# Gated linear attention with a channel mix: later loads for part of the weights and for the decays

## The chip, the cores and the metric

One NeuronCore of a Trainium2 chip runs the whole program. The metric is the device time of one execution in microseconds (us). TensorE (PE) does matmuls, VectorE (DVE), ScalarE (ACT) and GpSimd (POOL) work on tiles, and every transfer is issued by SyncE (SP), in the order in which its instructions stand, onto 16 DMA engines that share them.

## The reference

```python
def _attn_ref(q, k, v, f_logit):           # (4, 8, 768, 48) each
    f = 1.0 / (1.0 + np.exp(-f_logit))
    state = zeros(B, H, D, D)
    for t in range(S):
        state = f[:, :, t, :, None] * state + einsum('bhd,bhe->bhde', k[:, :, t], v[:, :, t])
        y[:, :, t] = einsum('bhd,bhde->bhe', q[:, :, t], state)

def _moe_ref(x, mu_k, mu_r, w_k, w_v, w_r):  # x = y as (4, 768, 384), d_ff = 1024
    x_prev = x shifted by one step
    xk = mu_k * x + (1 - mu_k) * x_prev
    xr = mu_r * x + (1 - mu_r) * x_prev
    k = maximum(xk @ w_k, 0)
    return sigmoid(xr @ w_r) * (k * k @ w_v)
```

Inputs and output are float32.

## The kernel before, in words

The 4 x 768 steps are cut into 24 chunks of 128 steps (`i`), six to a batch row; three chunks make a unit (`u`, 8 of them). A chunk is attention work (`add_attention`, L215), a unit is the mix and the three weight products (`add_mix`, L454). The work is written as named tasks with their engines, estimated costs, places and dependencies, and a planner (`Plan.schedule`, L84) picks one task after another by the earliest start that its own estimates give; the instructions of each engine then stand in that order. A task that gets a new dependency thus changes the order of others on every engine, and the number of filler matmuls.

The tasks of chunk `i` that matter here: `qk` loads q and k (512 KB, four buffers, so chunk 4 takes chunk 0's), `v` loads v (192 KB, three buffers); `b` scans the decays into running products; `q`, `kr`, `n`, `k` scale q and k (L250 to L272; `kr` on GpSimd, L258 and L259); `TR` transposes the keys on PE and `kt` copies them out (L314 and L315); `SP` makes scores and state sums (L325, L345); `m` masks the scores (L337), `za`, `zb`, `T` carry the state (L290, L296, L302); `YA` and `YB` are the output matmuls (L362), `w` lies between them (L381 and L382), `y` copies the result out (L394 on ScalarE or L396 on VectorE). The results of three chunks are spread into x by six small transfers (`sp`, L452).

The tasks of unit `u`: `d`, `xm`, `xh`, `xl` make the mixed inputs as a high and a low part (L464 to L497); `F0` to `F7` multiply by 128 columns of wk each (L505), `r`, `h`, `kk`, `l` square the relu into high and low parts (L528 to L543); `R0` to `R2` multiply by wr, `W` by wv in two halves; `sg` takes the sigmoid of that and of the decays of unit `u + 3` (L568, L571), `o` and `out` finish. `f{u}` loads the decays of a unit (768 KB, three buffers, L410).

Weights come as 64-bit words that are turned into a high and a low float part on the chip (`add_words`, L601). wk has 8 pieces of 384 KB (piece p is what F`p` reads), wv 6 of 512 KB through two buffers, wr 4. A piece is a load (L629), three VectorE steps S, T, X (L623, L632, L635), a ScalarE cast of the high part (L638) and the low part on GpSimd (L642). Late in the program the words are loaded again to be checked (`add_check`, L682), through the same two buffers.

Where the planner finds PE without work it puts in filler matmuls in fours (`fill`, L697).

Of the kernel before, what the change touches and what calls it, by code (L numbers as in the profile page):

```python
# [18 lines left out]
P = 128  # L19
# [3 lines left out]
UC = 3  # L23
# [8 lines left out]
NQ, NFB = 4, 3  # L32
# [159 lines left out]
class Rwkv:  # L192


    wk = wr = wv = None
# [205 lines left out]
    def add_unit(self, pl, u):  # L401

        nc = self.nc
        gates = [f"{n}{i}" for i in range(UC * (u - NFB), UC * (u - NFB + 1)) for n in "bg"
                 if i >= 0 and (n == "b" or i % NCH > 0)]
        ga = u - LEAD - GATE
        t = lambda cs=slice(0, UC): self.f_t[u % NFB][:, cs]

        def load(cs=slice(0, UC)):
            nc.sync.dma_start(self.f_t[u % NFB][:, cs], self.zt[u, :, cs])  # L410

        if u == 0:
            for c in range(UC):
                cs = slice(c, c + 1)
                pl.add(f"f0.{c}", ga - 0.4, ("Q", 0.71, 1, lambda cs=cs: load(cs)))
                pl.add(f"sf0.{c}", ga - 0.4, ("A", 0.63, 0, lambda cs=cs: nc.scalar.activation(t(cs), t(cs), AF.Sigmoid)),
                       after=[f"f0.{c}"] + ([f"sf0.{c - 1}"] if c else []))
        else:
            pl.add(f"f{u}", ga - 0.4 if u >= NFB else -1.5 + 0.1 * u, ("Q", 2.13, 1, load), after=gates)
            if u < NFB:  # L420
                def sf():
                    nc.scalar.activation(t(), t(), AF.Sigmoid)
                    if SPLIT and u == 2:
                        nc.scalar.preload_act_table_set(EXP_SET)

                pl.add(f"sf{u}", -1.0 if SPLIT and u == 2 else -9, ("A", 1.5 + 2.6 * (SPLIT and u == 2), 0, sf),
                       after=[f"f{u}", ("ex" if SPLIT else "sf1") if u > 1 else "sf0.2"])
            else:
                pl.add(f"sf{u}", u - 2.5, ("A", 0.0, 0, lambda: None), after=[f"sg{u - NFB}"])
        x, s = lambda: self.b("x", u), lambda: self.b("stage", u)  # L430
        ys = [f"y{i}" for i in range(UC * u, UC * u + UC)]
        for j in range(KJ):
            pl.add(f"sp{u}.{j}", u - PREP - 0.1, ("Q", 0.2, 2, lambda j=j: self.spread(x(), s(), j)), after=ys, uses=[("x", u), ("stage", u)])
        if u % NU == 0:
            pl.add(f"x0{u}", u - PREP, ("G", 0.1, 0, lambda: nc.gpsimd.memset(x()[:, :, 0:1], 0.0)),
                   uses=[("x", u)])
        else:
            pl.add(f"x0{u}", u - PREP, ("G", 0.36, 0, lambda: nc.gpsimd.tensor_copy(
                x()[:, :, 0:1], self.b("x", u - 1)[:, :, UT : UT + 1])),
                after=[f"sp{u - 1}.{j}" for j in range(KJ)], uses=[("x", u), ("x", u - 1)])  # L440
# [160 lines left out]
    def add_words(self, pl, clamp=False):  # L601
# [3 lines left out]
        nc = self.nc  # L605

        def piece(name, p, home, view, load, shape, hi, lo, first):
            place = WORDS[name][0] + WORDS[name][1] * p
            n = int(np.prod(shape))
            us = lambda per, at: per * n + at  # L610
            t_key = ("pm", (name, p))

            def t(dt=I32):
                a = self.b(*t_key)[:, :n].bitcast(dt)
                return a if len(shape) == 1 else a.rearrange("p (a b) -> p a b", a=shape[0])

            def shift():
                high = view()[..., 1]
                if clamp:
                    nc.scalar.activation(t(F32), high.bitcast(F32), AF.Abs)  # L620
                    nc.vector.tensor_scalar(t(F32), t(F32), 2.0**-15, None, op0=ALU.max)
                    high = t()
                nc.vector.tensor_scalar(  # L623
                    t(), high, 3, 0x3FFFFFFF, op0=ALU.logical_shift_left, op1=ALU.bitwise_and)

            low, high = lambda: view()[..., 0], lambda: view()[..., 1]
            x = lambda: low().bitcast(F32)
            tu = {"takes" if first else "uses": [home]}
            pl.add(f"{name}{p}", place - 0.4, ("Q", n * P * 8 / 370e3, 1, lambda: nc.sync.dma_start(view(), load())), **tu)  # L629
            dve = us(0.00104, 0.15)  # L630
            pl.add(f"{name}S{p}", place, ("V", dve, 0, shift), after=[f"{name}{p}"], takes=[t_key], uses=[home])
            pl.add(f"{name}T{p}", place, ("V", dve, 0, lambda: nc.vector.scalar_tensor_tensor(  # L632
                t(), low(), 29, t(), op0=ALU.logical_shift_right, op1=ALU.bitwise_or)),
                after=[f"{name}S{p}"], uses=[t_key, home])
            pl.add(f"{name}X{p}", place, ("V", dve, 0, lambda: nc.vector.scalar_tensor_tensor(  # L635
                low(), high(), -0x40000000, t(), op0=ALU.bitwise_and, op1=ALU.bitwise_or)),
                after=[f"{name}T{p}"], uses=[t_key, home])
            pl.add(f"{name}H{p}", place, ("A", us(0.00104, 0.12), 0, lambda: nc.scalar.copy(hi(), x())),  # L638
                   after=[f"{name}X{p}"], uses=[home])

            def sub(e):
                e.tensor_tensor(lo(), x(), hi().bitcast(F32), op=ALU.subtract)  # L642

            pl.add(f"{name}L{p}", place, ("G", us(0.00214, 0.2), 0, lambda: sub(nc.gpsimd)),
                   ("V", us(0.00104, 0.15), 1, lambda: sub(nc.vector)), after=[f"{name}H{p}"], uses=[home])


        for i, tag in enumerate(("k2h0", "k2l0", "k2h1", "k2l1")):
            for h in range(2):
                c = slice((2 * i + h) * P, (2 * i + h + 1) * P)  # L650
                home = ("words", ("wk", 2 * i + h)) if clamp else (tag, "w")

                def view(tag=tag, h=h, home=home):
                    if clamp:
                        w = self.b(*home)[:, : 2 * DM].bitcast(I32)
                        return w.rearrange("p (a n t) -> p a n t", a=KJ, t=2)
                    return self.words[tag][:, :, h * P : (h + 1) * P]

                piece("wk", 2 * i + h, home, view, lambda c=c: self.wk[:, :, c], [KJ, P],
                      *(lambda c=c, a=a: self.w["wk"][a][:, :, c] for a in (0, 1)), clamp or h == 0)  # L660
        nq = KJ * DM // 4
        for p in range(4):
            home = ("words", ("wr", p)) if clamp else ("lg", "w") if p < 2 else ("x", "w")
            at = 0 if clamp else p % 2 * nq

            def view(home=home, at=at):
                w = self.b(*home)
                w = w if len(w.shape) == 2 else w.rearrange(FL)
                return w[:, 2 * at : 2 * (at + nq)].bitcast(I32).rearrange("p (n t) -> p n t", t=2)

            c = slice(p * nq, (p + 1) * nq)
            piece("wr", p, home, view, lambda c=c: self.wr.rearrange("p a b t -> p (a b) t")[:, c], [nq],
                  *(lambda c=c, a=a: self.w["wr"][a].rearrange("p a b -> p (a b)")[:, c] for a in (0, 1)),
                  clamp or p % 2 == 0)
        for p in range(6):
            c = slice(p * 512, (p + 1) * 512)
# [5 lines left out]
    def add_check(self, pl):  # L682

        nc = self.nc
        pieces = [(w, slice(c, c + m)) for w, n, m in ((self.wk, KJ * DFF, 512), (self.wv, NF * DM, 512), (self.wr, KJ * DM, DM))
                  for c in range(0, n, m)]
        for p, (w, c) in enumerate(pieces):
            n = c.stop - c.start
            v = lambda p=p, n=n: self.b("words", ("c", p))[:, : 2 * n].bitcast(I32).rearrange("p (n t) -> p n t", t=2)
            pl.add(f"c{p}", CHECK[0] + CHECK[1] * p, ("Q", n * P * 8 / 370e3, 1, lambda v=v, w=w, c=c: nc.sync.dma_start(  # L690
                v(), w.rearrange("p a b t -> p (a b) t")[:, c])), takes=[("words", ("c", p))])
            pl.add(f"cm{p}", CHECK[0] + CHECK[1] * p + 1, ("V", 0.00104 * n + 0.15, 0, lambda v=v, p=p: nc.vector.tensor_reduce(
                self.least[:, p : p + 1], v()[..., 1].bitcast(F32), axis=mybir.AxisListType.X, op=ALU.min,
                apply_absolute_value=True)), uses=[("words", ("c", p))])
        return [f"cm{p}" for p in range(len(pieces))]
# [249 lines left out]
```

## Time and profile before

| | us |
|---|---|
| median of 3 runs | 357.24 (357.2 to 357.62) |
| profiled execution | 357.22 |
| its span | 355.1 |
| PE busy | 320.0 (90% of the span) |
| DVE busy | 260.3 (73%) |
| ACT busy | 201.5 (57%) |
| POOL busy | 196.5 (55%) |

The span is from the first to the last instruction of the profiled execution; some 2 us lie around it. Engines run side by side, so busy times don't add up; what an engine waits for is read from the stretch in which it waits. Matmul counts are passes: a float32 matmul that isn't marked otherwise shows as two.

### The profile page before, as it was taken

The numbers are of one execution on the slowest core, as the hardware profiler recorded it, in microseconds if no ns is written. First come the engines' busy times: TensorE is split into PE (matmuls) and PEld (weight loads), VectorE is DVE, ScalarE is ACT, GpSimd is POOL, SyncE is SP. The second block draws the span as 40 slices with busy tenths as digits, with TensorE's granted clock in tenths as the row PEclk, the third lists the DMA queues.
The fourth block names the chain that finished last, engine by engine and source line by source line (L and its number), as shares of the span: only waits on it lengthen the run. The fifth ranks groups of instructions, "written<-read, shape, count | busy, mean of one in ns | idle before, by whom it ended". The sixth has DMA issues, their size and how long they took to land.

```text
span 355.1 us, 10862 instructions
## 1 busy us (share of the span) xinstructions
PE 320.0 (90%) x4482; PEld 304.0 (86%) x4482; DVE 260.3 (73%) x526; ACT 201.5 (57%) x400; POOL 196.5 (55%) x235
## 2 busy tenths in 40 slices
PE   0294678999999999999999999999999999999993
PEld 0283567888989999999999999999999999999992
DVE  7887699989998798877999788848973943723110
ACT  3786358758367827844467537772676156605520
POOL 2555459985779357733677267725790634634400
PEclk9999899999999999999999999999999999999998
DMA  7999462336451363366323632131401100010001
GB/s 260 398 378 372 162 223 65 106 105 209 118 185 59 127 226 129 123 236 221 117 81 116 212 128 89 46 121 52 160 1 38 50 27 11 9 46 22 3 24 52
DMA packets 20650, 45.32 MB, mean 128 GB/s; under 512 B 2928, under 2 KB 13040, under 8 KB 20592
## 3 DMA queue, kind: packets, MB, share of 16 engines
q1 hardware_dynamic: 20592, 44.55, 37.0%
q8 instruction: 37, 0.61, 0.7%
q14 instruction: 21, 0.17, 0.1%
HBM read 38.64 MB, written 4.72 MB: 122 GB/s over the span
## 4 chain that ended last, share of the span: by engine, by line
PE 68%; DVE 13%; ACT 5%; issue 4%; DMA 3%; POOL 3%; SPq 1%; DVEq 0%; POOLq 0%; ACTq 0%
PE pm L505 55%; PE py L362 6%; PE pm L310 3%; PE pss L325 2%; DMA f<-in_zt 2%; DVE pm L632 2%; PE pss L345 2%; DVE pm L623 2%; POOL k2l L543 1%; DVE xm L482 1%; DVE ss L337 1%; DMA words<-in_wv 1%; DVE xm L477 1%; DVE words L635 1%; DVE xh L491 1%
## 5 line engine op out<-in xcount | busy, mean ns | idle before, releaser
L505 PE MATMUL pm<-xh,wk 128*128 128x384 f32 x384 | 105.3, 344 | 1.5 <-POOL wk L642 1.1
L505 PE MATMUL pm<-wv,k2h 128*128 128x384 f32 x384 | 98.6, 338 | 0.0
L543 POOL TENSOR_TENSOR k2l<-kk,k2h 128x384 fp32r<-128x384 f32 x64 | 68.5, 1075 | 32.2 <-DVE kk L535 16.3
L497 POOL TENSOR_TENSOR xl<-xm,xh 128x384 fp32r<-128x384 f32 x48 | 52.5, 1095 | 60.4 <-DVE xh L491 54.6
L505 PEld LDWEIGHTS pm<-xh,wk 128*128 128x128 f32 x384 | 69.8, 188 | 4.4 <-POOL wk L642 2.0
L505 PEld LDWEIGHTS pm<-wv,k2h 128*128 128x128 f32 x384 | 68.7, 188 | 0.3
L505 PE MATMUL pm<-xl,wk 128*128 128x384 f32 x192 | 64.6, 337 | 0.0
L505 PE MATMUL pm<-wv,k2l 128*128 128x384 f32 x192 | 64.5, 336 | 0.0
L528 ACT ACTIVATE r<-pm 128x384 f32<-128x384 f32 x54 | 26.5, 490 | 34.0 <-PE pm L505 33.3
L505 PE MATMUL pm<-wr,xh 128*128 128x384 f32 x144 | 38.0, 345 | 1.0 <-DVE words L635 0.9
L505 PEld LDWEIGHTS pm<-wv,k2l 128*128 128x128 f32 x192 | 36.1, 188 | 0.0
L595 DVE TENSOR_TENSOR o<-pm,lg 128x384 f32<-128x384 f32 x24 | 13.3, 553 | 31.1 <-PE pm L505 30.9
L505 PEld LDWEIGHTS pm<-xl,wk 128*128 128x128 f32 x192 | 36.1, 188 | 0.0
L535 DVE SCALAR_TENSOR_TENSOR kk<-pm,r 128x384 f32<-128x384 f32 x38 | 21.1, 554 | 20.0 <-ACT r L528 18.8
L533 ACT ACTIVATE k2h<-r 128x384 fp32r<-128x384 f32 x64 | 33.6, 524 | 3.5 <-DVE r L529 1.2
L240 DVE TENSOR_TENSOR_SCAN pm<-f,low 128x512 f32<-128x512 f32 x24 | 32.7, 1363 | 0.1
L362 PE MATMUL py<-qk,z 64*64 64x64 f32 x704 | 22.9, 230 | 10.0 <-issue 3.3
L362 PEld LDWEIGHTS py<-qk,z 64*64 64x64 f32 x704 | 16.4, 135 | 18.0 <-issue 8.8
L505 PEld LDWEIGHTS pm<-wr,xh 128*128 128x128 f32 x144 | 25.2, 188 | 1.9 <-DVE words L635 1.0
L482 DVE SCALAR_TENSOR_TENSOR xm<-pm,mu_sb,x 128x384 f32<-128x384 f32 x42 | 25.7, 612 | 0.7
L700 PE MATMUL py<-ident 128*128 128x64 f32 x72 | 10.8, 310 | 15.4 <-DMA ident<-in_cst 15.4
L505 PE MATMUL pm<-wr,xl 128*128 128x384 f32 x72 | 24.2, 336 | 0.0
(101 smaller groups left out, 559.2 us busy)
## 6 DMA issues: line engine op xcount, KB each, us to landing
qk<-in_qkt SPq DMA_DIRECT2D x24, 512.0 KB, 4.3
words<-in_wv SPq DMA_DIRECT2D x12, 512.0 KB, 3.9
f<-in_zt SPq DMA_DIRECT2D x7, 768.0 KB, 5.2
v<-in_vt SPq DMA_DIRECT2D x24, 192.0 KB, 3.1
out<-o SPq DMA_DIRECT2D x24, 192.0 KB, 2.6
words<-in_wk SPq DMA_DIRECT2D x6, 512.0 KB, 5.4
words_k2h<-in_wk SPq DMA_DIRECT2D x4, 384.0 KB, 8.6
words_k2l<-in_wk SPq DMA_DIRECT2D x4, 384.0 KB, 9.4
```

What stands on the lines that cost most here:

```text
L240: pl.add(f"b{i}", ga, ("V", 1.25, 1, lambda: nc.vector.tensor_tensor_scan(b().rearrange(FL), f().rearrange(FL), self.low.rearrange(FL), 1. ...
L310: nc.tensor.transpose(pk()[:, j], k()[:, j], self.ident)
L362: first[c, h] = nc.tensor.matmul(to, lhs, rhs, start=(c, h) not in first, stop=stop, skip_group_check=True)
L482: pl.add(f"xm{u}.{n}{j}", pr, ("V", 0.62, 0, lambda xm=xm, n=n, j=j: nc.vector.scalar_tensor_tensor(xm(), pm("d", u, j)[:, :UT], self.mu_s ...
L497: e.tensor_tensor(lo(), xm(), hi().bitcast(F32), op=ALU.subtract)
L505: nc.tensor.matmul(ps, lhs(a, j), rhs(bb, j), start=ends[0] and i == 0, stop=ends[1] and i == len(pr) - 1)
L528: pl.add(f"r{u}.{f}", kf, ("A", 0.5, 0, lambda r=r, ps=ps: nc.scalar.activation(r(), ps(), AF.Relu)), ("V", 0.56, 0, lambda r=r, ps=ps: nc ...
L533: pl.add(f"h{u}.{f}", kf, ("A", 0.53, 0, lambda r=r, hi=hi: nc.scalar.activation(hi(), r(), AF.Square)), after=[f"r{u}.{f}"], **kw)
L535: pl.add(f"kk{u}.{f}", kf, ("V", 0.56, 0, lambda r=r, ps=ps, kk=kk: nc.vector.scalar_tensor_tensor(kk(), ps(), 0.0, r(), op0=ALU.max, op1= ...
L543: e.tensor_tensor(lo(), kk(), hi().bitcast(F32), op=ALU.subtract)
L595: pl.add(f"o{u}.{t}", kv, ("V", 0.56, 0, lambda t=t, ps=ps, o=o: nc.vector.tensor_tensor(o(), ps(), lg()[:, t], op=ALU.mult)), after=[f"W{ ...
L700: self.nc.tensor.matmul(self.py[:, 0, 256:320], self.ident, self.ident[:, :64], start=False, stop=True, skip_group_check=True)
```

## The change

wk pieces 4 to 7 and wv pieces 1 to 5 may be placed only after the load of q and k of chunk 5. The load of the decays of unit 4 and of each later unit is placed only after the copy of the transposed keys of chunk 3(u - 3) + 4, which is chunk 7 for unit 4. The check loads are placed only after wv piece 5.

```diff
@@ add_unit
-            pl.add(f"f{u}", ga - 0.4 if u >= NFB else -1.5 + 0.1 * u, ("Q", 2.13, 1, load), after=gates)
+            pl.add(f"f{u}", ga - 0.4 if u >= NFB else -1.5 + 0.1 * u, ("Q", 2.13, 1, load), after=gates + ([f"kt{UC * (u - NFB) + 4}"] if u > NFB else []))
@@ add_words, piece
-            pl.add(f"{name}{p}", place - 0.4, ("Q", n * P * 8 / 370e3, 1, lambda: nc.sync.dma_start(view(), load())), **tu)
+            behind = ["qk5"] if not clamp and (name == "wk" and p >= 4 or name == "wv" and p >= 1) else []
+            pl.add(f"{name}{p}", place - 0.4, ("Q", n * P * 8 / 370e3, 1, lambda: nc.sync.dma_start(view(), load())),
+                   after=behind, **tu)
@@ add_check
-                v(), w.rearrange("p a b t -> p (a b) t")[:, c])), takes=[("words", ("c", p))])
+                v(), w.rearrange("p a b t -> p (a b) t")[:, c])), after=["wv5"], takes=[("words", ("c", p))])
```

Two lines are added, so that a line after L629 has a number higher by one to two in the changed kernel.

On SyncE, the loads from wk pieces 2 and 3 (`words_k2l0`) on. In the kernel before:

```order
L629 DMA words_k2l0_130<-in_wk 128x3x256 x2
L629 DMA words_k2h1_131<-in_wk 128x3x256
L629 DMA words1_121<-in_wv 128x1024
L629 DMA words_k2h1_131<-in_wk 128x3x256
L629 DMA words_k2l1_132<-in_wk 128x3x256 x2
L230 DMA v0_101<-in_vt 128x384
L228 DMA qk0_64<-in_qkt 128x1024
L230 DMA v1_102<-in_vt 128x384
L228 DMA qk1_65<-in_qkt 128x1024
L410 DMA f1_62<-in_zt 128x1536
L230 DMA v2_103<-in_vt 128x384
```

In the changed kernel:

```order
L630 DMA words_k2l0_130<-in_wk 128x3x256 x2
L230 DMA v0_101<-in_vt 128x384
L228 DMA qk0_64<-in_qkt 128x1024
L230 DMA v1_102<-in_vt 128x384
L228 DMA qk1_65<-in_qkt 128x1024
L630 DMA words_k2h1_131<-in_wk 128x3x256
L630 DMA words1_121<-in_wv 128x1024
L630 DMA words_k2h1_131<-in_wk 128x3x256
L630 DMA words_k2l1_132<-in_wk 128x3x256 x2
L230 DMA v2_103<-in_vt 128x384
L452 DMA x1_105<-stage0_107 16x384 x6
```

The buffers `words_k2h1` and `words_k2l1` hold wk pieces 4 to 7, `words1` wv piece 1. v of chunk 3 (`v0`), q and k of chunk 4 (`qk0`), v of chunk 4 (`v1`) and q and k of chunk 5 (`qk1`) now stand ahead of them, and the decays of unit 4 (`f1`) are gone from here.

On VectorE, from the state update of chunk 2 on, between the scan of chunk 5's decays and the mix of unit 0. In the kernel before:

```order
L302 TENSOR_TENSOR sm_77<-pss_87,z01_73 128x192
L623 TENSOR_SCALAR pm1_92<-words_k2h0_129 128x384
L632 SCALAR_TENSOR_TENSOR pm1_92<-words_k2h0_129,pm1_92 128x384
L382 COPY done_76<-py_88 128x2
L635 SCALAR_TENSOR_TENSOR words_k2h0_129<-words_k2h0_129,pm1_92 128x3x128
L623 TENSOR_SCALAR pm2_93<-words0_120 128x512
L337 TENSOR_TENSOR ss1_98<-pss_87,mask_69 128x512
L296 TENSOR_TENSOR z11_75<-pss_87,z10_74 128x4x48
L302 TENSOR_TENSOR sm_77<-pss_87,z11_75 128x192
L250 TENSOR_TENSOR qk0_64<-qk0_64,pm0_91 128x512
L270 TENSOR_TENSOR pm0_91<-rb0_95,pm0_91 128x512
L262 SCALAR_TENSOR_TENSOR qk0_64<-pm0_91,qk0_64 128x2x128
```

In the changed kernel:

```order
L302 TENSOR_TENSOR sm_77<-pss_87,z01_73 128x192
L250 TENSOR_TENSOR qk0_64<-qk0_64,pm0_91 128x512
L382 COPY done_76<-py_88 128x2
L270 TENSOR_TENSOR pm0_91<-rb0_95,pm0_91 128x512
L337 TENSOR_TENSOR ss1_98<-pss_87,mask_69 128x512
L396 TENSOR_SCALAR x1_105<-py_88 128x2x128
L396 TENSOR_SCALAR x1_105<-py_88 64x128 x2
L396 TENSOR_SCALAR stage0_107<-py_88 128x128
L296 TENSOR_TENSOR z11_75<-pss_87,z10_74 128x4x48
L302 TENSOR_TENSOR sm_77<-pss_87,z11_75 128x192
L262 SCALAR_TENSOR_TENSOR qk0_64<-pm0_91,qk0_64 128x2x128
L266 SCALAR_TENSOR_TENSOR qk0_64<-pm0_91,qk0_64 128x2x64 x2
```

Here `words_k2h0` is wk piece 1 and `words0` wv piece 0. The steps of wk piece 1 and the first of wv piece 0 have gone to places behind q and k of chunks 4 and 5; the copy of chunk 2's result (L396) has come over from ScalarE.

On PE, between YB of chunk 3 and YA of chunk 4. In the kernel before:

```order
L310 MATMUL pm1_92<-ident_68,qk0_64 128x128 x4
L325 MATMUL pss_87<-qk0_64 64x64 x16
L345 MATMUL pss_87<-v1_102,ktk0_99 48x48 x16
L310 MATMUL pm1_92<-ident_68,qk1_65 128x128 x4
L700 MATMUL py_88<-ident_68 128x64 x4
```

In the changed kernel:

```order
L310 MATMUL pm1_92<-ident_68,qk0_64 128x128 x4
L310 MATMUL pm0_91<-ident_68,qk1_65 128x128 x4
L325 MATMUL pss_87<-qk0_64 64x64 x16
L345 MATMUL pss_87<-v1_102,ktk0_99 48x48 x16
L702 MATMUL py_88<-ident_68 128x64 x20
```

The transposes of chunk 5 (`qk1`) have moved ahead of the scores and sums of chunk 4, and the fillers behind these have grown from 4 to 20.

## Rows read from the trace of the kernel before

**Rows 1.** The page: PE's busy tenths in 40 slices.

```profile
PE   0294678999999999999999999999999999999993
```

**Rows 2.** Windows: length; PE, PEld, DVE, ACT, POOL busy; PEclk; DMA; GB/s.

```profile
30.00:40.00 10.00, 5.12 (x249) 4.27 (x247) 7.35 (x15) 5.46 (x15) 5.01 (x8) 1.00 0.96 335
40.00:50.00 10.00, 7.22 (x206) 6.02 (x206) 7.86 (x20) 5.23 (x13) 3.08 (x5) 0.83 0.43 143
...
100.00:110.00 10.00, 10.00 (x160) 9.37 (x159) 9.15 (x20) 7.21 (x17) 8.58 (x10) 1.00 0.34 106
```

**Rows 3.** Chain that ended last: start us, us, what.

```profile
28.59 0.78 issue
...
33.41 2.49 issue
...
41.56 1.56 PE py L362 x48
```

**Rows 4.** Windows of 1 us, columns as in rows 2.

```profile
42.00:43.00 1.00, 1.00 (x44) 0.90 (x36) 0.27 (x1) 0.00 (x0) 0.00 (x0) 0.50 0.18 43
```

**Rows 5.** Timeline of SyncE: start us, us, line, transfer, count.

```profile
20.48 0.54 SPq L629 DMA_DIRECT2D words_k2h<-in_wk  x1
...
23.57 2.50 SPq L629 DMA_DIRECT2D words_k2l<-in_wk  x2
...
27.27 0.86 SPq L228 DMA_DIRECT2D qk<-in_qkt  x1
```

**Rows 6.** DMA of 22 to 28 us: packets; issue, KB, landing us.

```profile
DMA packets 1678, 2.20 MB, mean 367 GB/s; under 512 B 80, under 2 KB 1506, under 8 KB 1677
...
qk<-in_qkt SPq DMA_DIRECT2D x1, 512.0 KB, 9.1
```

**Rows 7.** Instructions on the tile qk, 0 to 50 us.

```profile
DMA to landing us min/median/max: 3.6/6.6/9.1
```

**Rows 8.** Timeline of PE and GpSimd: start, us, what [idle before <-releaser].

```profile
33.12 0.30 PE L362 MATMUL py<-qk,z 64*64 64x64 f32 x3 [0.58 <-DVE z L296]
35.90 0.39 PE L362 MATMUL py<-qk,z 64*64 64x64 f32 x11 [2.49 <-issue]
...
36.38 0.74 POOL L258 TENSOR_TENSOR qk<-qk,rb 128x256 f32<-128x256 f32 x1 [1.65 <-DMA qk<-in_qkt]
...
40.83 0.47 PE L362 MATMUL py<-qk,z 64*64 64x64 f32 x14 [1.23 <-POOL qk L258]
```

**Rows 9.** DMA queues, 33.4 to 35.9, then 40.9 to 43 us: packets, MB.

```profile
q8 instruction: 1, 0.02, 2.7%
...
q8 instruction: 1, 0.02, 3.6%
```

**Rows 10.** Timeline of VectorE: chunk 5's result copied out.

```profile
75.12 1.04 DVE L396 TENSOR_SCALAR x<-py 128x256 f32<-128x256 f32 x3
```

**Rows 11.** Timeline of 32 to 66 us, PE.

```profile
47.91 0.46 PE L362 MATMUL py<-qk,z 64*64 64x64 f32 x16 [0.93 <-DVE z L296]
...
51.33 0.44 PE L505 MATMUL pm<-xh,wk 128*128 128x384 f32 x1
...
54.61 1.89 PE L700 MATMUL py<-ident 128*128 128x64 f32 x16
```

**Rows 12.** Timeline of GpSimd: low parts of wk 2, wk 7, wv 3.

```profile
56.53 1.03 POOL L642 TENSOR_TENSOR wk<-words_k2l,wk 128x384 fp32r<-128x384 f32 x1
...
68.83 1.02 POOL L642 TENSOR_TENSOR wk<-words_k2l,wk 128x384 fp32r<-128x384 f32 x1 [0.23 <-ACT wk L638]
...
71.06 2.33 POOL L642 TENSOR_TENSOR wv<-words,wv 128x512 fp32r<-128x512 f32 x1
```

**Rows 13.** Timeline of ScalarE: the square behind F0.0.

```profile
55.12 0.53 ACT L533 ACTIVATE k2h<-r 128x384 fp32r<-128x384 f32 x1
```

**Rows 14.** Timeline of PE: R0.1.

```profile
75.26 0.62 PE L505 MATMUL pm<-wr,xh 128*128 128x384 f32 x2 [0.87 <-DVE words L635]
```

**Rows 15.** Timeline of ScalarE: the sigmoid of unit 4's decays.

```profile
122.64 1.47 ACT L571 ACTIVATE f<-f 128x1536 f32<-128x1536 f32 x1
```

## Prediction

> **What bounds the kernel now.** I read the page's slices first, then 10 us windows, the chain of waits, and last the timeline of 14 to 100 us by engine. From slice 11 on PE is at 9 tenths in every slice but the last [rows 1], and a window there has no idle PE at all [rows 2]: after about 100 us the time is PE's work, and a change can only help by letting that stretch begin earlier. Before it PE is half idle (5.12 us of the 10 from 30 on, then 7.22), while the DMA engines are full (share 0.96, then 0.43) [rows 2]. So the question is how much earlier the first big matmul can start, and whether the start that it wins survives to 100 us.
>
> [...]
>
> **The part that is moved forward.** wk pieces 4 to 7 and wv piece 1 are 4 x 384 + 512 KB = 2.1 MB, issued from 20.48 to 26.07 [rows 5]. At the 367 GB/s of that stretch they are 5.7 us of transfer [rows 6]. q and k of chunk 4, issued at 27.27, land 9.1 us later [rows 5, 6]; the quickest such load takes 3.6 [rows 7]. Nothing else of the issue time moves: v of chunk 3 goes out just ahead of them in either order, since it waits for chunk 0's output matmuls. So chunk 4's keys land at about 31 instead of 36.4, and GpSimd's wait of 1.65 us for them [rows 8] goes. By itself that wait was not what PE waited for.
>
> PE's stall at 33.41 is. It falls after 3 of 16 passes of one task [rows 8], and a 0.02 MB packet of an instruction queue starts inside it [rows 9]. I counted the passes of the program from the start: the stalls at 28.59 [rows 3], at 33.41 and before 40.83 [rows 8] lie 126 passes apart, each a weight load and a matmul, so 252 instructions. I take each to be a wait for the next block of code, asked for when the block before it was entered. Its transfer shares the full DMA engines: from entry to entry it took 6.5 us for the block needed at 33.4 (29.4 to 35.9) and 4.9 for the next (35.9 to 40.8). With the engines nearly empty the packet after that starts within 2.1 us of the entry, and PE has no stall for it [rows 9]. [...]
>
> In the changed order the engines run nearly dry between 26.8 and 31, so that the block needed at 33.4 comes at 33.4 to 34.3; I take 33.9, a stall of 0.5. But the moved 2.1 MB now go out at 32 to 35 us, behind chunk 5's q and k, and keep the engines full to about 40. The next block is asked for at 33.9, in that stretch. With 4.0 to 6.6 us it comes between 37.9 and 40.5; I take 39.3. So **the stall is moved to the next block** more than removed.
>
> Step by step from there: YA2's rest, chunk 3's scores and sums, and YB2 end at 36.1; chunk 2's result is copied out by VectorE, 1.35 us as for chunk 5 now (1.04 us [rows 10] and a last short piece), to 37.5 (before, by ScalarE); YA3 starts and halts after two passes until 39.3 (before 40.83); YB3 ends at 41.2, at the lower clock, since PE is again idle for some 3 us, against 43.12. Term one: **-1.9 us**; bounds -3.5 (block in time, full clock) and 0.
>
> **The part that is put in between.** From YB3's end to the first matmul of unit 0's F0.0 it is 8.2 us now (43.12 to 51.33) [rows 3, 11]. In the new order chunk 4's key transposes are copied by ScalarE behind chunk 3's result, and only then come its scores: 1.35 + 0.5 + 1.3 = 3.2 us by the same tasks' lengths around 44 us. Then 20 fillers stand there instead of 4. A filler is two passes; 16 passes took 1.89 us [rows 11], so 40 take 4.7. Behind them YA4, SP5 and YB4 need 2.3 us without waits (from 47.91 to 51.33 with waits now [rows 11]). Together 10.2. VectorE is no later: piece 1 of wk now stands before the mix of unit 0, and by its steps z of chunk 4, which YA4 needs, is ready 7.4 us after YB3. Term two: **+2.0**; bounds +1.5 (VectorE alone) and +2.6 (fillers begun at the lower clock).
>
> From F0.0 to the low half of wk piece 2, which F0.2 waits for, it is 6.2 us (51.33 to 57.56 [rows 11, 12]). Now ScalarE casts wv piece 0 ahead of F0.0's relu; in the changed order the relu, which needs F0.0's end, and the square (0.53 us [rows 13]) stand first, and GpSimd's row of low halves waits for that cast: 1.6 + 0.2 + 1.1 to it, 0.7 for it, and 1.3 + 1.0 + 1.0 on GpSimd make 6.9 to 7.0. Term three: **+0.8**, bounds 0 and +1.2. From there to wk piece 7 (56.53 to 69.85) GpSimd goes from one to the next almost without a gap, in nearly the same order in both programs, so a lag is kept.
>
> Behind that there is slack. PE sits idle 0.87 us before R0.1 [rows 14], where it waits for a bank that VectorE frees, and VectorE is ahead of GpSimd in the new order; the low half of wv piece 3 took 2.33 us, where wk's, three quarters of its size, take 1.02 [rows 12]; it ran beside a scan of VectorE, which it would now miss. Term four: **-0.9**, bounds -1.0 and 0.
>
> **The rest.** The decays of unit 4 leave the full stretch and go out behind chunk 10's keys, where those of unit 5 stand now, before 100 us; the sigmoid that reads them runs at 122.64 [rows 15], so even a load of 9 us as above is covered with 10 to spare. If they slipped by more than that, ScalarE would hold unit 4. The check loads already stand behind wv piece 5. From unit 1 on PE's order is the same apart from units 4 and 5, where it changes between chunk and big matmuls twice more: **+0.2**, an estimate at 0.1 each from fractions of a microsecond of idle PE in a whole window of such changes [rows 2]; bounds 0 and 0.6.
>
> The sum is -1.9 + 2.0 + 0.8 - 0.9 + 0.2 = +0.2 us on the profiled execution's 357.22, which is within 0.02 of the median: **357.4 us**. A difference under 0.2%, 0.7 us, cannot be told from none.
>
> **Rivals.**
> (1) *The code comes in time and the clock stays up.* The request at 33.9 may meet engines that have only just filled again, or be made earlier. YB3 then ends at 39.6, and the other terms leave -1.4: 355.8 us. For it: with the engines nearly empty no block was late [rows 9]. Against: nothing was in flight then, and here 2.1 MB are. 0.30.
> (2) *The stall at 33.4 does not depend on the backlog.* If a block of code takes its turn beside the data, it took its 6.5 us for its own reasons and takes them again. Then YA2 goes on at 35.9, YB3 ends at 43.1, term one is 0, and the fillers and the new order cost their 2 us: 359.3. It decides if YA2's third pass comes after 35. [...] Against it stands that the packet ran 4 us or more after the entry at 29.4 with full engines, and within 2.1 us of the entry at 40.8 with nearly empty ones [rows 8, 9]. 0.17.
> (3) *The next block comes at 40.5 and YB3 runs at the lower clock*, to 42.4: term one is -0.7, the sum +1.4, 358.6 us. 0.13.
> The change does what it says: the order of the loads shows it. That all is hidden behind PE is excluded by PE's idle time before 60 us.
>
> **Numbers.** Forecast 0.37, rivals 0.30, 0.17 and 0.13; 0.03 for a gain from elsewhere. Faster 0.33, same 0.37, slower 0.30. The range 355.5 to 358.9 takes in (1), (3) and half of (2); the forecast's own is 356.8 to 357.9.
>
> **What would show it.** Chunk 4's q and k land before 32 us; PE's 2.49 us of issue at 33.4 shrink under 1; a new stall after two passes of YA3, until 38 to 40.5; YB3's end near 41; 40 filler passes in a row up to about 49; F0.0 at 51 to 52; the low half of wk piece 7 ready at 70 to 71; R0.1 at 75 to 76. I am wrong if F0.0 starts before 50 or after 53, or if PE shows more than 1 us of new idle time after 100 us.

## The result, and the profile after

The changed kernel takes 360.49 us (median of 5 runs, 358.88 to 363.12) against 357.24 for the kernel before: **0.76% slower**, ratio 1.0076 (95% interval 1.0046 to 1.0105). The prediction, 357.4 us in a range of 355.5 to 358.9, was wrong. A second series gave 1.0057 (1.0036 to 1.0078).

The profile that came with the result is of the longest run, 363.12 us; the second series gave a profile of a run near the median, 360.90 us. Both are read here, since they lose the time by two different chains of waits. The page of the first profile, PE's busy tenths and granted clock in 40 slices:

```profile
PE   0496689988999999999999999999999999999993
PEclk9999667999999999999999999999999999999998
```

Windows of the first profile, columns as in [rows 2]:

```profile
40.00:50.00 10.00, 8.41 (x141) 7.79 (x142) 4.95 (x11) 5.07 (x12) 1.86 (x2) 0.67 0.72 228
50.00:60.00 10.00, 10.00 (x145) 9.74 (x145) 8.18 (x17) 1.50 (x6) 4.89 (x7) 0.57 0.17 43
...
120.00:130.00 10.00, 10.00 (x177) 9.64 (x176) 9.08 (x22) 6.50 (x9) 4.75 (x6) 1.00 0.13 33
```

The second of these windows in the kernel before:

```profile
50.00:60.00 10.00, 8.94 (x100) 8.10 (x97) 9.69 (x19) 6.88 (x16) 8.75 (x9) 1.00 0.39 127
```

PE is busier between 40 and 60 us than before (7.22 us of the first 10 [rows 2]), and yet later: it is busy at a granted clock of 0.67 and 0.57, where it had 0.83 and 1.00; the first two are means of windows in which it changes (by windows of 1 us it is 0.50 from 39 to 44 and from 49 to 58, and 1.00 from 45 to 48). VectorE, 7.86 of 10 us before [rows 2], is down to 4.95. From the first output tile on the loss hardly changes: that tile's last VectorE step, at 86.8 us before, is 6.4 us later, the last tile's 6.2; in the second profile 3.3 and 3.4. As predicted, the question is only when the full stretch begins.

PE's timeline, first profile:

```profile
33.28 0.64 PE L362 MATMUL py<-qk,z 64*64 64x64 f32 x14 [0.58 <-DVE z L296]
...
37.25 0.33 PE L362 MATMUL py<-qk,z 64*64 64x64 f32 x2 [1.76 <-DVE z L296]
39.06 0.70 PE L362 MATMUL py<-qk,z 64*64 64x64 f32 x14 [1.48 <-issue]
...
46.58 0.30 PE L345 MATMUL pss<-v,ktk 64*48 64x48 f32 x8 [1.57 <-issue]
46.82 7.49 PE L702 MATMUL py<-ident 128*128 128x64 f32 x40
...
57.35 0.69 PE L505 MATMUL pm<-xh,wk 128*128 128x384 f32 x1
```

PE's timeline, second profile:

```profile
41.35 0.57 PE L362 MATMUL py<-qk,z 64*64 64x64 f32 x14 [2.58 <-issue]
...
47.37 0.30 PE L345 MATMUL pss<-v,ktk 64*48 64x48 f32 x8 [1.11 <-issue]
47.60 4.68 PE L702 MATMUL py<-ident 128*128 128x64 f32 x40
...
53.94 0.45 PE L505 MATMUL pm<-xh,wk 128*128 128x384 f32 x1
```

The stall of 2.49 us at 33.41 [rows 3] is gone, and a new one stands after two passes of chunk 3's first output matmuls, as forecast. A third, not forecast, stands 126 passes on, after 24 of chunk 4's 32 sum passes. The profile shows nothing that PE waits for in them ("issue"). That it is a block of code was the prediction's reading, and I keep it as one: no trace names the cause. The 40 filler passes took 4.68 us in the second profile, at 1.00, and 7.49 in the first, where the clock was 0.50 for most of them, as in this window of the first profile:

```profile
50.00:51.00 1.00, 1.00 (x7) 1.00 (x6) 0.97 (x3) 0.06 (x1) 0.71 (x2) 0.50 0.05 16
```

What the prediction had not looked at is the spread of unit 0: six transfers of 24 KB each that put the results of chunks 0 to 2 into x, and for which the mix waits. Rows of the kernel before: the spread's time from issue to landing (instructions on the tile x, 30 to 60 us), ScalarE's first step of the mix, and VectorE's mask of chunk 4:

```profile
DMA to landing us min/median/max: 1.9/2.3/3.4
...
44.36 0.58 ACT L474 ACTIVATE pm<-x,mu_sb 128x384 f32<-128x384 f32 x1
...
46.91 0.68 DVE L337 TENSOR_TENSOR ss<-pss,mask 128x512 f32<-128x512 f32 x1
```

The same in the first profile of the changed kernel:

```profile
DMA to landing us min/median/max: 4.1/6.2/7.3
...
46.51 1.09 ACT L474 ACTIVATE pm<-x,mu_sb 128x384 f32<-128x384 f32 x2 [3.22 <-DMA x<-stage]
47.12 0.61 DVE L477 SCALAR_TENSOR_TENSOR xm<-x,one_mu,pm 128x384 f32<-128x384 f32 x1 [3.06 <-ACT pm L474]
...
51.54 0.68 DVE L337 TENSOR_TENSOR ss<-pss,mask 128x512 f32<-128x512 f32 x1
```

The spread is issued 0.9 us earlier than before (38.31 against 39.25), with the 2.1 MB of moved weights ahead of it, and ScalarE's first step on it comes 2.15 us later. Chunk 4's mask, which in the new order stands behind three parts of the mix, comes 4.6 us later.

The chain that ended last, second profile (`SPq` is SyncE issuing a transfer):

```profile
38.49 0.80 SPq L452
39.35 6.46 DMA x<-stage
45.92 0.38 ACT pm L474
...
51.02 0.60 DVE ss L337
```

Here the chain runs through the spread and VectorE, and PE's stall of 2.58 us is not on it. In the first profile it runs through PE:

```profile
37.58 1.48 issue
...
45.01 1.57 issue
...
46.89 7.42 PE py L702 x40
```

### The profile page after: what moved, and what is told of

Read it like the earlier page. It is cut to its first block, busy times and chain, and to the rows that moved or that the text cites. A ratio compares the mean times of both kernels' runs of the same rounds, so it can differ in the third digit from the quotient of the medians.

```text
span 361.0 us, 10931 instructions
## 1 busy us (share of the span) xinstructions
PE 329.9 (91%) x4514; PEld 315.1 (87%) x4514; DVE 262.8 (73%) x528; ACT 200.3 (55%) x398; POOL 195.0 (54%) x235
## 4 chain that ended last, share of the span: by engine, by line
PE 84%; DVE 7%; POOL 2%; issue 2%; DMA 2%; ACT 1%; DVEq 0%; ACTq 0%
PE pm L505 64%; PE py L362 8%; PE pss L325 4%; PE pm L310 4%; PE py L702 3%; PE pss L345 3%; DVE pm L240 2%; DMA words<-in_wv 1%; DVE pm L634 1%; POOL wk L644 1%; DVE pm L623 1%; DMA lg<-in_wr 1%; POOL wv L644 1%; DVE qk L250 1%; POOL k2l L543 1%
## 5 line engine op out<-in xcount | busy, mean ns | idle before, releaser
L505 PE MATMUL pm<-wr,xh 128*128 128x384 f32 x144 | 37.9, 344 | 1.4 <-DVE words L637 1.4
L505 PEld LDWEIGHTS pm<-xl,wk 128*128 128x128 f32 x192 | 36.2, 189 | 0.0
L240 DVE TENSOR_TENSOR_SCAN pm<-f,low 128x512 f32<-128x512 f32 x24 | 33.9, 1414 | 0.0
L702 PE MATMUL py<-ident 128*128 128x64 f32 x104 | 17.9, 347 | 14.3 <-DVE pm L240 14.3
L702 PEld LDWEIGHTS py<-ident 128*128 128x128 f32 x104 | 17.5, 260 | 14.5 <-issue 14.3
L362 PEld LDWEIGHTS py<-qk,z 64*64 64x64 f32 x704 | 17.2, 142 | 13.4 <-issue 7.1
L362 PE MATMUL py<-qk,z 64*64 64x64 f32 x704 | 23.7, 238 | 5.7 <-DVE z L296 2.3
L394 ACT ACTIVATE x<-py 64x128 f32<-64x128 f32 (+1 forms) x51 | 15.8, 310 | 23.3 <-PE py L362 22.5
```

Source lines behind the costliest of these rows:

```text
L240: pl.add(f"b{i}", ga, ("V", 1.25, 1, lambda: nc.vector.tensor_tensor_scan(b().rearrange(FL), f().rearrange(FL), self.low.rearrange(FL), 1. ...
L362: first[c, h] = nc.tensor.matmul(to, lhs, rhs, start=(c, h) not in first, stop=stop, skip_group_check=True)
L394: e.activation(o, i_, AF.Copy, scale=-1.0)
L505: nc.tensor.matmul(ps, lhs(a, j), rhs(bb, j), start=ends[0] and i == 0, stop=ends[1] and i == len(pr) - 1)
L702: self.nc.tensor.matmul(self.py[:, 0, 256:320], self.ident, self.ident[:, :64], start=False, stop=True, skip_group_check=True)
```

## The experiments

All on the changed kernel, if nothing else is said; ratios are against the kernel before in the same series.

### The changed kernel once more

> The changed kernel once more, for a second profile: its first one took 363.1 us, the median of its runs is 360.5. Theory A (the six transfers that spread chunk results into x land 6.2 us after issue instead of 2.3 because they are queued behind the 2.1 MB of moved weights; the mix of unit 0, which stands ahead of chunk 4's mask on VectorE, waits for them, and chunk 4's output matmuls wait for the mask): the spread again lands about 6 us after issue, chunk 4's mask starts at 50 to 52 and F0.0 at 55 to 58 in this profile too; time 359 to 361. Theory C (the whole loss is the lower clock of 48 to 58 us of the first profile, 7.5 us instead of 4.7 for 40 filler passes and about 1 us for what stands behind them): a profile with the full clock there has F0.0 at about 53.5 and takes 357.5 or less; the clock, not the spread, tells slow and quick runs apart.

Measured: 360.14 us, ratio 1.0057 (1.0036 to 1.0078). The spread landed 5.8 us after issue, the mask started at 50.94, F0.0 at 53.94 (the expectation said 55 to 58). Theory C falls: the fillers ran at a granted clock of 1.00 (every window of 1 us from 47 to 53), and the run still took 360.90 us, 3.7 more than the run of the profile of before.

### Without 16 of the 20 fillers

```diff
-                    fw = "P", 0.88, 0, lambda: self.filler(4)
+                    ahead = last_p if last_p != "FILL" else ahead; fw = "P", 0.88, 0, (lambda: None) if last_p == "FILL" and ahead == "SP4" else lambda: self.filler(4)
```

> The changed kernel with 16 of the 20 filler matmuls behind chunk 4's sums left out, all else in its order. Theory A: chunk 4's output matmuls wait for VectorE and GpSimd (z of chunk 4 was ready at 53.6, the fillers ended at 54.3), so F0.0 moves by under 1 us and the time stays at 359 to 361, or is longer if the idle PE gets the lower clock. Theory B (the forecast's term two: PE itself is what the 40 passes hold up): chunk 4's output matmuls start 3.8 us (full clock) to 6 us (lower clock) earlier, F0.0 at 51 to 53, and the time falls to 355 to 357.

Measured: 360.33 us, ratio 1.0054 (1.0036 to 1.0073), the same as with them. PE's timeline:

```profile
46.81 1.10 PE L702 MATMUL py<-ident 128*128 128x64 f32 x8
51.77 0.71 PE L362 MATMUL py<-qk,z 64*64 64x64 f32 x16 [3.86 <-DVE z L296]
54.89 0.69 PE L505 MATMUL pm<-xh,wk 128*128 128x384 f32 x1
```

PE now sits idle for 3.86 us and waits for VectorE. So in this kernel the fillers were cover over a wait, and theory B, that PE's own passes hold it up there as the forecast's term two has it, falls. Without them the passes from 51.77 to F0.0 took 3.1 us, at a granted clock of 0.50, against 1.7 at 1.00 in the second profile (52.21 to 53.94). F0.0 came 1.0 us later than there, and the time is the same.

### The mask ahead of the mix

```diff
-                        after=["onemu", f"x0{u}"], takes=[("xm", (u, n, j))], uses=[("pm", ("d", u, n, j))] + xs)
+                        after=["onemu", f"x0{u}"] + (["T4"] if u == 0 else []), takes=[("xm", (u, n, j))], uses=[("pm", ("d", u, n, j))] + xs)
```

> The changed kernel with one more dependency: the mix of unit 0 may be placed only behind chunk 4's state update, so that chunk 4's mask and state stand ahead of the mix on VectorE, and the planner puts in 4 fillers there, not 20. Theory A: the mask starts as soon as the scores are there (45 to 46 instead of 51.5) and chunk 4's output matmuls run at about 48; F0.0 then waits for the low parts of the mix on GpSimd (52.7) and starts at 53 to 54, 3 to 4 us earlier than in the profile of the changed kernel; time 357 to 358.5. Theory C: the clock is as low as before, and with PE idle for longer F0.0 stays at 55 or later; 359 to 361.

Measured: 362.95 us, ratio 1.0149 (1.0113 to 1.0186): a miss. The part up to F0.0 went as theory A has it, and further: the mask started at 45.87 and F0.0 at 50.88. But the planner also put the rest of units 0 and 1 in another order, with PE switching otherwise among wv's matmuls: 1.0 us behind before at the first output tile, 4.8 at the fourth. This run says that the order on VectorE counts up to F0.0; on the total it says nothing, since two things changed.

### The moved loads behind the spread

```diff
-            behind = ["qk5"] if not clamp and (name == "wk" and p >= 4 or name == "wv" and p >= 1) else []
+            behind = ["sp0.2"] if not clamp and (name == "wk" and p >= 4 or name == "wv" and p >= 1) else []
```

> The changed kernel with the moved weights (wk pieces 4 to 7, wv piece 1) issued behind the six spread transfers of unit 0 instead of ahead of them; every other engine has the same order. Theory A and the code theory (a block of 126 passes' code comes late when the DMA engines are full): the spread lands about 2.3 us after issue, the mix starts at 43 to 44 instead of 46.5, PE has no stall of over 0.5 us after two passes of chunk 3's first output matmuls (1.48 us before) nor behind 24 of chunk 4's 32 sum passes unless the weights are in flight there (1.57 us before), F0.0 at 50 to 53; time 355.5 to 358. Theory B (the fillers alone): the fillers still take 40 passes behind chunk 4's sums, F0.0 follows them 3 us later, at about 52 if they run at the full clock and 55 if not; 357 to 360. If the stalls of PE stay where they were with the engines empty, the code theory falls.

Measured: 357.31 us, ratio 0.998 (0.9963 to 0.9997). Every engine but SyncE has the order of the changed kernel, and SyncE's differs by the place of five loads: **the whole loss is gone**. PE's timeline, and the spread's landing:

```profile
38.94 0.60 PE L362 MATMUL py<-qk,z 64*64 64x64 f32 x16 [1.76 <-DVE z L296]
43.70 4.68 PE L702 MATMUL py<-ident 128*128 128x64 f32 x40
49.38 0.46 PE L362 MATMUL py<-qk,z 64*64 64x64 f32 x16 [1.00 <-DVE z L296]
51.27 0.44 PE L505 MATMUL pm<-xh,wk 128*128 128x384 f32 x1
```

```profile
DMA to landing us min/median/max: 1.9/2.7/3.6
```

Chunk 3's 16 passes run in one piece, no stall of "issue" of over 0.3 us is left between 24 and 76 us, and F0.0 is back at the time of before [rows 11].

### The five loads right ahead of the spread

```diff
-        return order
+        late = [o for o in order if o[0] in ("wk4", "wv1", "wk5", "wk6", "wk7")]; rest = [o for o in order if o not in late]; at = [o[0] for o in rest].index("sp0.0"); return rest[:at] + late + rest[at:]
```

> The changed kernel with the five moved loads issued two places later, behind v of chunk 5 and right ahead of the spread; all else in the same order. It parts the two gates that came together: the block of code that chunk 3's output matmuls need is asked for at about 33, when the DMA engines now have little to do, but the spread stands behind all of the 2.1 MB. If the late spread alone is enough (theory A): no stall of over 0.5 us in chunk 3's first output matmuls, the spread lands 5 us or more after issue, the mix starts at 46 to 49, F0.0 at 54 to 57, 0.4 to 1.2% slower than before. Rival (the late block of code alone made the loss): F0.0 at 51 to 52.5 and the time within 0.2% of before.

Measured: 362.85 us, ratio 1.0144 (1.0109 to 1.0178): slower than expected, and slower than the change. PE, then ScalarE:

```profile
37.33 0.61 PE L362 MATMUL py<-qk,z 64*64 64x64 f32 x16 [1.76 <-DVE z L296]
43.12 4.68 PE L702 MATMUL py<-ident 128*128 128x64 f32 x40
52.89 0.71 PE L362 MATMUL py<-qk,z 64*64 64x64 f32 x16 [5.08 <-DVE z L296]
...
55.81 0.45 PE L505 MATMUL pm<-xh,wk 128*128 128x384 f32 x1
```

```profile
46.86 1.09 ACT L474 ACTIVATE pm<-x,mu_sb 128x384 f32<-128x384 f32 x2 [5.57 <-DMA x<-stage]
```

PE has no stall of over 0.3 us of its own any more, and ScalarE waits 5.57 us for the spread. The late spread alone is enough to make the loss. That the loss is larger than the change's comes in part from the clock: the mix starts 0.9 us later than in the second profile (45.92 there), and after the idle 5.08 us PE's passes up to F0.0 run at 0.50 and take 2.9 us instead of 1.7, so that F0.0 is 1.9 us later than there.

### 1.28 MB of the 2.1 MB ahead of the spread

```diff
-            behind = ["qk5"] if not clamp and (name == "wk" and p >= 4 or name == "wv" and p >= 1) else []
+            behind = (["sp0.2"] if name == "wk" and p >= 6 else ["qk5"]) if not clamp and (name == "wk" and p >= 4 or name == "wv" and p >= 1) else []
```

> The changed kernel with 768 KB of the moved 2.1 MB (wk pieces 6 and 7) issued behind the spread, 1.28 MB still behind chunk 5's q and k; all else in the same order. Theory (both gates are the length of the backlog): the 1.28 MB are through at about 38.5 to 39.5, so that the stall in chunk 3's first output matmuls is 0.3 to 1.5 us, the spread lands 2.3 to 3.5 us after issue, F0.0 comes at 51.3 to 52.5, and the time lies between that of the changed kernel and that with all five behind the spread: from 0.1% below to 0.3% above before. Rival (any of these loads behind chunk 5's q and k costs the same): 0.5% slower, as the change.

Measured: 359.72 us, ratio 1.0039 (1.0015 to 1.0062), between the two as the theory has it, but above its range. The spread landed 3.4 us after issue, and no engine waited for it; F0.0 came at 53.80, not by 52.5. What the expectation had too small is the stall:

```profile
37.17 0.33 PE L362 MATMUL py<-qk,z 64*64 64x64 f32 x2 [1.75 <-DVE z L296]
40.35 0.70 PE L362 MATMUL py<-qk,z 64*64 64x64 f32 x14 [2.86 <-issue]
```

The chain that ended last runs through it and through the fillers behind it, and not through the spread:

```profile
37.49 2.86 issue
...
46.47 4.61 PE py L702 x40
...
53.20 0.71 PE py L362 x30
```

So the other gate is enough by itself too: with the spread in time, the stall of 2.86 us makes a loss of 0.39%, and here the fillers are PE's own time. The length of the backlog does not set this gate in proportion: from the start of the task in which the block before was entered (33.28) PE needed 7.1 us behind 1.28 MB, and 5.8 and 6.7 behind 2.1 MB.

### Twelve more passes at the start

```diff
-        pl.add(f"TR{i}", at, ("P", 0.44, 0, tr), after=I("k") + ["cst"], takes=[("pm", ("k", i))])
+        pl.add(f"TR{i}", at, ("P", 0.44, 0, tr if i else lambda: (self.fill(6), tr())), after=I("k") + ["cst"], takes=[("pm", ("k", i))])
```

> The changed kernel with 6 more filler matmuls (12 passes) ahead of chunk 0's key transposes, where PE waits for VectorE anyway; all else in the same order. Code theory (every 126 passes PE needs the next block of its code, and with full DMA engines that block is late): the stall that stood after 2 of 16 passes of chunk 3's first output matmuls (1.48 and 2.58 us in the two profiles) is gone from there and stands 12 passes earlier, after 22 of the last 32 passes of chunk 2's output matmuls; the one after 24 of chunk 4's 32 sum passes (1.57 and 1.11 us) stands after 12 of them. Rival (the stall belongs to the instruction at which it is seen, by a wait that the profile does not show): both stay at their old passes. Time in either case 359 to 361, as the changed kernel.

Measured: 364.87 us, ratio 1.0202 (1.017 to 1.0233). PE:

```profile
33.97 0.29 PE L345 MATMUL pss<-v,ktk 64*48 64x48 f32 x4 [1.66 <-issue]
43.41 0.58 PE L362 MATMUL py<-ss,v 64*48 64x64 f32 x10 [4.77 <-issue]
```

The stall is gone from behind the first two passes of chunk 3 and stands ahead of the last 10 of chunk 2's 32 passes, 12 passes earlier, as the code theory says. The one behind chunk 4's sums did not come (when the block before had been entered, at 43.41, the DMA share was 0.16 and 0.08 in the two windows of 1 us up to 45), and the time is a miss: the stall was 4.77 us, not 1.5 to 2.6, and everything behind it came later with it, the spread too, which nobody waited for once it was issued (1.9 us to landing). DMA queues of 34 to 38, then of 38 to 42 us:

```profile
q1 hardware_dynamic: 608, 1.16, 93.2%
```

```profile
q1 hardware_dynamic: 1062, 1.19, 92.1%
q8 instruction: 1, 0.02, 1.5%
```

The block before was entered at 33.97; in the next 4 us no packet of an instruction queue moved at all, beside 608 packets of data. By windows of 0.1 us the packet of q8, which I take for the code, starts at 41.0, and PE goes on 2.4 us behind it. Three other stalls have about the same distance: packets at 31.5 here and at 36.2 and 44.2 in the first profile start 2.3 to 2.8 us before PE goes on. What differs is the time from the entry of a block to the start of the next one's packet: 7.0 us here with the engines full (share 0.93 and 0.94), and 1.1 us after 43.41, with a share of 0.28 from 42 to 44. When the packet was asked for, no trace shows.

### The two halves of the change

Without the dependency of the decays:

```diff
-            pl.add(f"f{u}", ga - 0.4 if u >= NFB else -1.5 + 0.1 * u, ("Q", 2.13, 1, load), after=gates + ([f"kt{UC * (u - NFB) + 4}"] if u > NFB else []))
+            pl.add(f"f{u}", ga - 0.4 if u >= NFB else -1.5 + 0.1 * u, ("Q", 2.13, 1, load), after=gates)
```

> The change without its dependency of the decays: the weights stand behind chunk 5's q and k as in the changed kernel, the decays of unit 4 (768 KB) go out where they did before, now right behind the weights and ahead of the spread. The planner puts 4 fillers and the mask of chunk 4 ahead of the mix here. Theory A (backlog ahead of the spread): the spread lands 6 to 9 us after issue, VectorE waits for it though chunk 4's mask is early, F0.0 at 52 to 55; the loss of the whole change comes from this part: 0.3 to 1% slower than before. Rival (the decays' part costs the time): no slower than before by over 0.2%.

Measured: 360.81 us, ratio 1.0084 (1.0059 to 1.011). With another 768 KB ahead of it the spread landed 6.0 us after issue (9.5 at most), and F0.0 started at 52.55:

```profile
47.75 2.10 ACT L474 ACTIVATE pm<-x,mu_sb 128x384 f32<-128x384 f32 x4 [3.32 <-DMA x<-stage]
```

F0.0 is only 1.2 us later than before, the first output tile 2.7. Behind F0.0 VectorE waits for a load of wv in both, 0.51 us there (up to 80.19) and 0.66 before (up to 77.13). That run has its own order on every engine, and what of its loss is order is not shown.

Without the dependency of the weights (and the check loads' one):

```diff
-            behind = ["qk5"] if not clamp and (name == "wk" and p >= 4 or name == "wv" and p >= 1) else []
+            behind = []
...
-                v(), w.rearrange("p a b t -> p (a b) t")[:, c])), after=["wv5"], takes=[("words", ("c", p))])
+                v(), w.rearrange("p a b t -> p (a b) t")[:, c])), takes=[("words", ("c", p))])
```

> The change without its dependency of the weights: only the decays of unit 4 and on wait for the later keys. Theory A: PE's, VectorE's and ScalarE's orders up to 70 us are those of before, 0.77 MB less stands ahead of the spread, PE's stalls are as before (2.49 us at 33.4); the time is that of before within 0.2%, at best 0.3% faster. Rival (the later loads of decays hold up the units behind): 0.5% or more slower.

Measured: 357.15 us, ratio 0.9973 (0.9955 to 0.999). The two halves add up to the whole within their intervals: +0.84% and -0.27% make +0.57%, and the second series of the changed kernel has +0.57%. Where the 0.27% come from is not settled: the one profile of this kernel is of its longest run, 358.62.

### Less work on VectorE, twice

With the loads behind the spread VectorE is busy 41.6 of the 44 us from 34 to 78 us. So chunk 2's result was given back to ScalarE, first with the planner free to put the rest in a new order:

```diff
-        pl.add(f"y{i}", at, ("A", 1.2, 0, lambda: y_out(nc.scalar)), ("V", 1.2, 0, lambda: y_out(nc.vector)),
+        pl.add(f"y{i}", at, ("A", 1.2, 0, lambda: y_out(nc.scalar)), *((("V", 1.2, 0, lambda: y_out(nc.vector)),) if i != 2 else ()),
```

> The weights behind the spread of unit 0 as in the third experiment of that name, and chunk 2's result copied out by ScalarE, not by VectorE, as in the kernel before; the planner then puts chunk 4's mask ahead of the mix and 8 fillers behind chunk 4's output matmuls. Theory D (with the backlog gone VectorE is the bound: 41.6 us busy of the 44 from 34 to 78, and R0.1 waits 1.6 us for a step of wv on it): 1.35 us less of work on VectorE brings F0.0 to 49 to 50.5 and R0.1 to 75 to 75.5 (76.5 before); time 0.4 to 0.8% below that of before. Rival (GpSimd's row of low parts is the bound from 54 us on): F0.0 earlier but R0.1 at 76 or later; 0.2% below before as without this edit.

Measured: 357.49 us, ratio 0.9997 (0.9972 to 1.0021). R0.1 came at 73.81, 1.45 us earlier than before [rows 14]; the first output tile was 1.3 us ahead, the tenth level, the last 0.3 behind. The gain went in units 2 and 3, whose order on PE the planner had changed. Then with only the copies of that result (three to x, one to the stage) moved, and all else in its place:

```diff
-            order.append((n, way, slot))
+            order.append((n, self.tasks[n][2][0] if n == "y2" else way, slot))
```

> All five moved loads behind the spread, and chunk 2's result copied out by ScalarE at the same place in the order, with no other instruction moved on any engine. Theory D (VectorE bounds 34 to 78 us there): 1.35 us less on VectorE, R0.1 at 75.0 to 75.5 against 76.5, and since PE's order behind it is kept, all of it stays to the end: 0.4 to 0.7% below before. Rival (given back, as in the run in which the planner put everything in a new order: 1.3 us ahead at 87 us, 0.3 behind at the end): within 0.2% of before.

Measured: **356.13 us, ratio 0.9947** (0.9919 to 0.9976), faster than both kernels. ScalarE and PE:

```profile
36.47 0.97 ACT L394 ACTIVATE x<-py 128x256 f32<-128x256 f32 x3 [1.61 <-DVE ss L337]
```

```profile
75.83 0.62 PE L505 MATMUL pm<-wr,xh 128*128 128x384 f32 x2 [1.37 <-DVE words L637]
```

Chunk 4's mask starts at 47.08 against 48.39 with the loads behind the spread alone, and R0.1 at 75.83 against 76.50: in this profile, of one of the longer runs (357.50), half of the expected 1.35 us arrives there.

## Why the prediction was wrong

The steps in the prediction's order, each profile against the profile of before (times in us; terms rounded one by one):

| term | before | forecast | first profile | second profile |
|---|---|---|---|---|
| one: end of chunk 3's output matmuls | 43.12 | -1.9 | 41.58: -1.5 | 43.74: +0.6 |
| two: from there to F0.0 | 8.21 | +2.0 | 15.77: +7.6 | 10.20: +2.0 |
| three: F0.0 to F0.2's second weights | 6.28 | +0.8 | 7.46: +1.2 | 6.91: +0.6 |
| four: from there to R0.1 | 17.65 | -0.9 | 17.38: -0.3 | 18.18: +0.5 |
| the rest | | +0.2 | -1.0 | -0.1 |
| sum | | +0.2 | +5.9 | +3.7 |

F0.0 starts after 53 in both, which the prediction had named as a sign of being wrong.

- **Right:** what bounds the kernel; that chunk 4's q and k come early (GpSimd starts on them at 31.99 and 32.70, not 36.38; forecast about 31); that the stall at 33.4 goes and comes back one block of 126 passes on; term three; that the late loads of the decays cost nothing.
- **Term one: a size that was off.** I let the next block come at 39.3, between 37.9 and 40.5. It let PE go on at 39.06 and 41.35 in the two profiles, at 40.35 behind only 1.28 MB, and at 43.41 with twelve passes more. From the entry of the block before, that is 5.8, 6.7, 7.1 and 9.4 us, where I took 4.0 to 6.6. The forecast followed the stall to one further block; there was a third, of 1.57 and 1.11 us. The sum also has chunk 3's last 48 output passes at the lower clock, for which it names some 3 us of idle PE; no run shows that idle time of this length brings it. They took 1.56 us at 0.50 before [rows 3, 4] and in both profiles, and 0.91 at 1.00 with the loads behind the spread; with the loads right ahead of it the clock fell during them (0.74, then 0.50) though PE's wait ahead of chunk 3 was only 1.76 us.
- **Term two: the step that failed is "VectorE is no later".** It counted VectorE's own instructions, and not the transfers that the mix waits for. The prediction has the moved 2.1 MB keep the DMA engines full to about 40; that the spread goes out at 38, behind them, it leaves out. It landed 6.2 and 5.8 us after issue in the two profiles in place of 2.3, and z of chunk 4, forecast for 7.4 us after the end of chunk 3's output matmuls, was ready 10.9 and 8.1 us after it. The loads behind the spread undo the whole loss; the loads right ahead of it, without a stall of PE, make it 1.4%. That the second profile's term two is right is chance: chunk 3's matmuls end so late there, by term one, that the spread's delay hides behind them and the fillers, which end at 52.28 when z of chunk 4 is ready at 51.9. With the block of code in time the miss moves from term one to term two: in the run with the loads right ahead of the spread chunk 3's matmuls end at 39.58 (-3.5), and from there to F0.0 it is 16.2 us (+8.0). Either gate alone costs time: the spread there, the block of code behind 1.28 MB, where nobody waited for the spread and 0.39% was lost.
- **The fillers** were priced as PE's work (4.7 us). Left out, nothing was gained. In the first profile they fell to 0.50 after 1.5 us and stayed there; the upper bound of +2.6 allowed only for their beginning at it. They ended at 54.31, 1.8 us after z of chunk 4 was ready (52.5), and the 2.3 us of matmuls behind them took 3.0. That is the first profile's alone; the median does not hang on it.
- **Term four failed:** the slack of 0.87 us was not taken up but grew to 1.38 and 1.63. I had GpSimd's low part of wv piece 3 miss VectorE's scan. VectorE came later along with GpSimd, and the two met again, in the second profile as before [rows 12] (the scan started at 71.07 there; the low parts of wv at 62.08 and 67.28, without a scan beside them, took 1.34 and 1.32 us):

```profile
74.07 2.32 POOL L644 TENSOR_TENSOR wv<-words,wv 128x512 fp32r<-128x512 f32 x1
74.07 1.22 DVE L240 TENSOR_TENSOR_SCAN pm<-f,low 128x512 f32<-128x512 f32 x1
```

- **The rivals.** (2) had the time nearly right (359.3) by the wrong way: the stall at 33.4 is gone. Against its rule, that a block takes its turn beside the data, stand the 4 us with 608 packets of data and none of an instruction queue (34 to 38, with twelve passes more), if the block is asked for when the one before it is entered. When it is asked for, no trace shows. (3) was close on the next block (40.5). None had the spread. On the code, the stall that moved by exactly 12 passes, and the next one that did not come at a DMA share of 0.16 and 0.08, side with blocks of 126 passes; that a block is fetched one ahead was my estimate, which no trace shows.

## What to carry to other kernels

When a load is moved, list every transfer that it is now ahead of, the smallest first: here six transfers of 24 KB on the same queue came late behind 2.1 MB (6.2 us to landing, not 2.3), and so, as I read PE's stalls of up to 2.86 us, did a block of code on another; that cost more than the earlier load of 512 KB gained. A filler or a stall that the chain names can be cover over another wait: leave it out, or put the suspected traffic elsewhere with all else in its place, before it is priced. And in a planned kernel an edit can change the order far behind it: here 1.3 us won at the start were lost that way, and a gain remained when the order was held fixed.

## What was not expected of the hardware

- PE went on with what I read as its next block of code, a packet of 0.02 MB of q8, up to 9.4 us after it had entered the block before (33.97 to 43.41), at a DMA share of 0.93 and 0.94. The packet itself started 7.0 us after that entry; at a share of 0.28 the next one started 1.1 us after it (43.41 to 44.5). From the packet's start to PE's next pass it was 2.3 to 2.8 us in four stalls (two with twelve passes more, two in the first profile).
- The clock fell to 0.50 at 38.0 in the first profile, after PE had been mostly idle from 35.5, rose at 44.9, fell again at 48.3, after another 1.57 us without work, and stayed there to 58.5 (by windows of 0.1 us), although PE was busy without a gap from 46.6 on. In the kernel with the loads behind the spread the same 40 passes ran at 1.00.
